# Linear attention and an MLP in one kernel: stripes 2 and 3 take k by v and the output product over the whole TensorE array, under a new order of the list

## The chip, the cores and the metric

The kernel runs on one core of one Trainium2 chip. The metric is device time in microseconds of one execution; lower is better. The engines are TensorE (PE, with its weight loads shown apart as PEld), VectorE (DVE), ScalarE (ACT), GpSimd (POOL) and the queue that issues most transfers (SP). Each has its own instruction stream, worked through in order, and semaphores hold an instruction until what it needs is there.

## The reference, cut to what matters

There are 4 batches and 8 heads, 768 positions, a head dimension of 64. The attention is linear, with a decay: within a block it is a masked product, and a state of 64x64 per head carries the earlier blocks.

```python
for b in range(nb):
    intra = np.einsum('bhic,bhjc->bhij', qb, kb) * Dmask[None]
    intra = np.einsum('bhij,bhjd->bhid', intra, vb)
    inter = np.einsum('bhid,bhde->bhie', qb * lam_pow[None], kv_state)
    out[:, :, sl] = intra + inter
    kb_dec = kb * rev_pow[None]
    kv_state = lam_block[None, :, None, None] * kv_state + np.einsum('bhsd,bhse->bhde', kb_dec, vb)
...
h = x @ w_in
g = np.where(pos, h, np.where(neg, 0.0, (h + beta) ** 2 / (4.0 * beta)))
return (g @ w_out).astype(np.float32)
```

The attention's output, 3072 rows of 512, is the x of the MLP: 512 to 2048 to 512, with a smooth ReLU between (beta is 1). The kernel takes blocks of 128 positions where the reference has 64; the result is the same function. Products are taken in bf16 and accumulated in float32.

## The kernel before

**Tiling.** The 24 blocks of 128 rows are cut into eight stripes of 4, 2, 3, 3, 3, 3, 3 and 3 blocks (`STRIPES`, line 25). The heads go in pairs, hp 0 to 3; a unit is a stripe and a pair, so `S21` is the scores of stripe 2, pair 1. A stripe's attention is followed by its MLP, in 16 parts of the hidden layer and one output block per block of rows.

**The order.** Nothing is scheduled by a tool. `ORDER` (lines 29 to 71) is a list of words, and the loop at line 574 issues the instructions of each word on their engines in that order. Each engine goes through its own words strictly in that order, so a word that waits holds every later word of its engine. The words:

- `L21k`: load k (or q, v) of stripe 2, half 1, issued by SP. `W0` to `W7`: the weights, issued by POOL (W0 to W3 a quarter of w_in each, W4 to W7 of w_out). `W4@L10q` makes the first transfer of the one wait until the last of the other has landed.
- `k21g`, `q21d`, `v21a`: scale k or q by its decay, or copy v, into bf16; the last letter is the engine (g POOL, d DVE, a ACT).
- `T`, `Q`: transpose k or q of a unit (on PE in stripes 0 to 3, by a DMA in 4 to 7); `t`, `u`: ACT takes the transposes out of PSUM.
- `S`, `s`: scores on PE, mask on DVE. `R`, `r`: k by v on PE (`att_r`, line 361), the state's step on DVE (line 404). `O`, `o`: output on PE (`att_o`, line 409), copied out by ACT. `X`: transpose of the output by a DMA (stripes 4 to 7).
- `P03`, `h03`: part 3 of stripe 0's hidden layer (PE, line 503) and its ReLU (ACT, line 526); `K` is the same for the first three parts, one pair of heads at a time. `A`: the rest of the activation for four parts (DVE, lines 482 to 485). `Y012`: part 2 of the four parts of output block 1 of stripe 0 (PE, line 535); `y` copies it out, `U` stores it.
- `B`: a mask. `E`: the table of decays for stripe 0's scan. `G`: zeros in a kq tile. `D2`: two matmuls on the identity whose result nobody reads (line 491).

**Two forms of the attention.** In stripes 0 to 3 two heads of 64 are packed into the array: k by v and the output product write PSUM partitions 0 to 63 for one head and 64 to 127 for the other, so they use half of the columns each (64 columns of weights, `128*64` in the trace), the state's part also half of the rows (`64*64`), the scores half of the rows (`64*128`):

```python
nc.tensor.matmul(po[p0:p0 + 64, c, :],
                 lhsT=d["vc"][:, hi, c, :], rhs=d["sc"][:, hi, c, :],
                 start=(c == 0), stop=(prior[c] is None), skip_group_check=True)
...
nc.tensor.matmul(po[p0:p0 + 64, c, :], lhsT=prior[c][p0:p0 + 64, :],
                 rhs=d["qT"][p0:p0 + 64, c * 128:(c + 1) * 128], ...)
```

In stripes 4 to 7 (`whole`) zeros stand between the heads in the tile of k, and every product uses the whole array (`128*128`); the state is then 128x128 with zeros off its two diagonal blocks, and the output comes out with rows on partitions, which the DMA of `X` transposes.

**PSUM.** There are four banks for the MLP (`pmm`, also taken by `D`), two for transposes, k by v and output (`pat`), two for one unit's scores (`psp`).

**The words around the change on POOL**, from the first weight load on: W0@L03v, W1@L01k, v03g, W2, W3@L03q, W4@L10q, v11g, q11g, W5, k13g, W6, W7, v12g, q20g. And on PE after stripe 0's first ten P words: P0b, P0c, Q12, Q10, T12, P0d, T10, P0f, T13, P0e, T11, S10, D1, Q13, D1, Q11, Y010.

Of the kernel before, what the change touches and what calls it, by code (L numbers as in the profile page):

```python
# [23 lines left out]

STRIPES = [(0, 0, 4), (0, 4, 2), (1, 0, 3), (1, 3, 3), (2, 0, 3), (2, 3, 3), (3, 0, 3), (3, 3, 3)]
# [4 lines left out]
D2 B1a E D1 D1 B0a D2 D2 L00q D1 L01v L02q L00k D2 L01k L03v q02g L00v k00a B3a q00g k01g L01q  # L30
Q00 L02v T00 D2 q01g v02g t00 u00 L02k Q02 T01 S00 L03q u02 t01 D1 L03k D1 B2a D2 Q01 s00 u01
v00d k02d S01 W0@L03v D2 s01 T02 R00 D2 D2 r00 L11q q03d t02 R02 W1@L01k v03g v01a O00 S02
L10v@W1 r02 k03d o00 R01 r01 s02 Q03 T03 t03 u03 D2 W2 W3@L03q O01 o01 S03 O02 q12d s03 R03 D1
r03 o02 K01 K02 L10q@W2 O03 o03 K00 K03 h01 L10k@W2 L11k@W1 h02 h00 P05 P03 P09 P0a h03 h05 h0a
W4@L10q P08 A00 P06 v11g q11g W5 h09 v10a P07 P04 h06 L11v@W3 k13g q10d h08 k11d P0b P0c Q12
k12d h07 Q10 T12 h0b P0d h04 L20q@W5 u12 t12 q13d k10d T10 P0f T13 u10 P0e L20k W6 t10 T11 h0d
t13 S10 D1 L21q W7 Q13 h0c A01 v12g q20g D1 v13d h0f h0e Q11 Y010 Y020 u13 s10 t11 u11 R11 R10
S11 Y030 s11 r11 r10 Y011 Y031 S12 O10 R12 A02 Y000 Y021 o10 Y012 R13 Y001 L20v@W1 A03 L21k@W1
r12 s12 Y032 r13 L30q Y022 O11 S13 L21v O12 k21a Y023 Y033 L31k L30k L31v k20g L31q o11 o12 y02
Q20 s13 Y013 y03 O13 Y002 v20g o13 u20 y01 q21g P12 h12 T20 k22g q22d q30g P10 P1a P15 h10 Q21  # L40
h1a U03 t20 P17 P11 h15 S20 R20 P13 k30g h17 k23d v21a L30v q23d Y003 u21 h13 T21 r20 h11 P14
P18 T22 s20 h14 t21 y00 v23g Q22 u22 A10 P16 O20 h16 v22d h18 D2 t22 o20 P1b P19 P1e A11 P1f T23
R21 h1b h19 S21 h1e h1f r21 q32g P1c s21 Q23 P1d h1d A12 h1c u23 Q30 v31g Y100 Y101 S22 t23 R23
Y110 k31a r23 T30 Y102 u30 Y111 Y112 s22 S23 k32a U02 L40k O21 v30g t30 o21 R22 A13 Y103 s23 r22
S30 O23 s30 v33g O22 o23 v32d Y113 o22 L40q R30 R31 P24 h24 r31 r30 G40 k33g q31d P20 R32 y11
# [12 lines left out]
L70k R53 r60 P45 S61 h45 y31 P4f X52 L70q O60 v63a o60 P4a P4e X51 h4f h4a r53 Y410 Y400 A41 O53
o53 q71g Y420 h4e A42 Y411 R61 A43 U32 Y421 Y401 Y412 Y402 R62 X53 s61 Y413 P57 k72a Y403 h57
T63 L70v k70g r61 r62 y41 P51 h51 P5a S62 s62 P50 O61 y40 v73d Y422 R63 P53 k73a h50 o61 h53 S63  # L60
h5a s63 k71g q70g P52 U40 v72d P58 Y423 T71 O62 h52 y42 P59 P54 h59 h54 T70 P56 h56 P5b r63 P55
O63 A50 S70 h55 o62 o63 q73d s70 P5d R73 P5f h58 r73 R72 U41 X61 U22 P5e h5d h5b h5f v70a h5e
U31 X62 P5c Y500 X63 A51 X60 A52 Y510 R70 h5c Y501 S71 Y511 P60 P63 h63 Y512 h60 Y502 A53 P68
q72g T73 r72 s71 Y503 Y513 P62 h68 v71g h62 T72 P61 y51 h61 S72 P67 R71 P6a P65 h67 h6a s72 r70
P6b h6b P66 U51 O72 y50 P69 A60 S73 r71 P6f o72 s73 h66 P64 X72 O71 h6f h69 P6d Y520 o71 Y521
h6d O70 P6c A62 o70 X71 h64 O73 Y522 h65 h6c P6e Y523 Y610 Y600 A61 o73 h6e A63 y52 X70 Y611
Y612 U42 Y601 Y602 X73 P75 Y613 Y603 y61 P78 P70 y60 h78 h75 P76 h76 P7b h7b P73 Y620 P71 U50
h73 h70 P72 U52 P7a U61 h71 P79 Y621 h72 h7a h79 Y622 A72 Y623 P74 h74 y62 P77 P7e h77 h7e P7d
P7f A70 P7c h7d h7f h7c U60 Y710 A71 Y700 Y711 Y701 Y712 U62 A73 Y713 Y702 Y703 y71 y70 U71 U70
Z72  # L70
# [8 lines left out]
def kernel(  # L79
# [63 lines left out]
    def load(s, n, which):  # L143
# [9 lines left out]
        if which == "q" and s < S_WH:  # L153
            return [nc.sync.dma_start(out=t.rearrange("p h c d -> p h (c d)"),
                                      in_=src.rearrange("h (p c) d -> p h (c d)", c=C))]
# [78 lines left out]

    kq_tiles = [const.tile([128, 9, 128], BF16, name=f"kq{i}") for i in range(NZ)]

    def kq_tile(u):
        return kq_tiles[(NP * u[0] + u[1]) % NZ]

    def set_zeros(u):  # L240
        C = shape(u[0])[0]
        z = kq_tile(u)[:, 0:2 * C, :].rearrange("p (c h) e -> p c h e", h=2)
        for hi in range(2):
            nc.gpsimd.memset(z[:, :, hi, (1 - hi) * D:(2 - hi) * D], 0.0)


# [10 lines left out]
    def att_cast(u, which, eng):  # L257

        s, hp = u
        C, T, first, last, whole = shape(s)  # L260
        src = raw[s, which][:, 2 * hp:2 * hp + 2, 0:C, :]
        d = st.setdefault(u, {})
        if which == "v":
            d["vc"] = bfp.tile([128, 2, CM, D], BF16, name="vc", tag="vc")
            dst = d["vc"][:, :, 0:C, :]
            if eng == "a":
                nc.scalar.copy(out=dst, in_=src)
            else:
                (nc.gpsimd if eng == "g" else nc.vector).tensor_copy(dst, src)  # L269
            return  # L270
        kq = d["kq"] = kq_tile(u)
        if which == "k" and whole:

            ap = list(kq[:, 0:2 * C, 0:D].ap)
            dst = bass.AP(kq.tensor, kq.offset, [ap[0], [128 + D, 2], [256, C], [1, D]])
        else:
            c0 = 0 if which == "k" else 2 * C if whole else C
            dst = kq[:, c0:c0 + C, :].rearrange("p c (h d) -> p h c d", h=2)
        row = 0 if which == "k" else Q1 if whole else {4: Q4, 2: Q2, 3: Q3}[C]
        inner = which == "q" and not whole  # L280
# [13 lines left out]

    def att_t(u, i):

        s, hp = u
        C, T, first, last, whole = shape(s)
        d = st[u]
        if "kqT" not in d:  # L300
            d["kqT"] = trp.tile([128, 9, 128], BF16, name="kqT", tag="kqT")
        if whole:
            nc.sync.dma_start_transpose(out=d["kqT"], in_=d["kq"].rearrange("p c e -> p (c e)"))
            return
# [18 lines left out]
    def att_s(u):  # L323

        s, hp = u
        C, T, first, last, whole = shape(s)
# [3 lines left out]
        for c in range(C):  # L330
            for hi in range(2):
                o = ps[:, hi, c * 128:(c + 1) * 128]
                if whole:
# [18 lines left out]
    def before(u):  # L352

        s, hp = u
        C, T, first, last, whole = shape(s)
# [4 lines left out]

    def att_r(u):

        s, hp = u
        C, T, first, last, whole = shape(s)
        d = st[u]
        n = C - 1 if last else C
        if whole:
# [5 lines left out]
        else:  # L373
            d["pk"] = pk = pat.tile([128, CM, D], F32, name="pk", tag="pat")
            d["ss"] = ssp.tile([128, CM, D], BF16, name="ss", tag="ss")
        for c in range(n):
            for hi in range(2):
                if whole:
                    nc.tensor.matmul(pk[:, c, hi, :],
                                     lhsT=d["kq"][:, 2 * c + hi, :], rhs=d["vc"][:, hi, c, :],  # L380
                                     start=True, stop=True)
# [4 lines left out]
                                 start=True, stop=True)  # L386

    def att_state(u):

        s, hp = u  # L390
        C, T, first, last, whole = shape(s)
# [7 lines left out]
        for c in range(C - 1 if last else C):  # L399
            kv = d["pk"][:, c, :, :].rearrange("p h e -> p (h e)") if whole else d["pk"][:, c, :]  # L400
# [7 lines left out]

    def att_o(u):

        s, hp = u
        C, T, first, last, whole = shape(s)
        d = st[u]
        if s not in x_tiles:
            x_tiles[s] = xpool.tile([128, KO, TM], BF16, name="xT", tag="xT")
        prior = [before(u)] + [d["ss"][:, :, c] if s == 0 else d["ss"][:, c, :]
                               for c in range(C - 1)]
        if whole:
            d["xn"] = xnp.tile([128, 3 * BLK], BF16, name="xn", tag="xn")
# [3 lines left out]
        for c in range(C):  # L423
            for hi in range(2):
                if whole:
# [10 lines left out]
        for c in range(C):  # L436
            if prior[c] is None:
                continue
            if whole:
# [10 lines left out]
    def att_out(u):  # L450

        s, hp = u
        C, T, first, last, whole = shape(s)
        d = st[u]
        if whole:
# [5 lines left out]
    def att_x(u):  # L461

        s, hp = u
        C, T = shape(s)[:2]
# [179 lines left out]
```

## Time and profile before

| what | value |
| --- | --- |
| time, median of 3 runs | 227.57 us (227.45 to 227.84) |
| the profiled execution's own time | 228.49 us |
| its span, first to last instruction | 226.8 us |
| mean granted TensorE clock | 0.985 |
| DMA | 35.95 MB, mean 159 GB/s |
| L503, hidden layer on PE | 500 matmuls, 91.1 us busy |
| L535, output layer on PE | 368 matmuls, 87.6 us busy |
| L526, ReLU on ACT | 128 instructions, 70.2 us busy |

How to read it: the span is cut into 40 equal slices, and a digit is the busy share of a slice in tenths. PEclk is the granted TensorE clock in the same slices. In a timeline a row has the start, the time to the end of the last of its instructions, engine, line, operation, tiles and shape, how many instructions were merged, and in brackets how long the engine had been idle and what ended that. The end of a matmul is modelled and overlaps the next one's start, so what a matmul takes of PE's stream is read from start to start. A row of a view by line has busy time, mean ns of one, and idle time before. In a view of stretches each engine has its busy time and count, and the last three numbers are the granted clock, the DMA share and GB/s.

### The profile page before, as it was taken

The numbers are of one execution on the slowest core, as the hardware profiler recorded it, in microseconds if no ns is written. First come the engines' busy times: TensorE is split into PE (matmuls) and PEld (weight loads), VectorE is DVE, ScalarE is ACT, GpSimd is POOL, SyncE is SP. The second block draws the span as 40 slices with busy tenths as digits, with TensorE's granted clock in tenths as the row PEclk, the third lists the DMA queues.
The fourth block names the chain that finished last, engine by engine and source line by source line (L and its number), as shares of the span: only waits on it lengthen the run. The fifth ranks groups of instructions, "written<-read, shape, count | busy, mean of one in ns | idle before, by whom it ended". The sixth has DMA issues, their size and how long they took to land.

```text
span 226.8 us, 4443 instructions
## 1 busy us (share of the span) xinstructions
PE 216.1 (95%) x1703; PEld 121.8 (54%) x1703; DVE 144.9 (64%) x233; ACT 125.9 (56%) x264; POOL 50.7 (22%) x89
## 2 busy tenths in 40 slices
PE   7389999999999999999999999999999999999994
PEld 2146444444775465555654666556654565455453
DVE  1059267792489767989399775991799486404930
ACT  5555487305986277985553666616681576074620
POOL 4672019123351435000313340024010000000000
PEclk9769999999999999999999999999999999999999
DMA  4999989999998699439999799999945103220112
GB/s 117 233 250 166 209 201 144 195 265 225 216 265 206 150 182 223 112 74 207 191 206 151 180 236 156 180 214 232 198 111 105 46 17 101 93 95 3 46 46 93
DMA packets 100630, 35.95 MB, mean 159 GB/s; under 512 B 89217, under 2 KB 97665, under 8 KB 100609
## 3 DMA queue, kind: packets, MB, share of 16 engines
q1 hardware_dynamic: 96384, 31.47, 63.9%
q0 software_dynamic: 4224, 4.19, 12.1%
q8 instruction: 13, 0.21, 0.4%
q14 instruction: 9, 0.07, 0.1%
HBM read 27.27 MB, written 6.29 MB: 148 GB/s over the span
## 4 chain that ended last, share of the span: by engine, by line
PE 73%; DMA 13%; SPq 5%; DVE 4%; ACT 1%; POOL 1%; issue 1%; DVEq 0%; POOLq 0%
PE py L535 31%; PE ph L503 28%; DMA w_in_sb<-in_moe_w_in_dram 5%; SPq L158 3%; DMA kqT<-kq 2%; DMA k_nat<-in_k_dram 2%; PE ps L334 2%; DMA xT<-xn 2%; DMA v_nat<-in_v_dram 2%; PE pt L310 2%; PE py L555 2%; PE po L432 1%; PE po L446 1%; PE ps L338 1%; DVE gT L485 1%; DVE ww L484 1%
## 5 line engine op out<-in xcount | busy, mean ns | idle before, releaser
L526 ACT ACTIVATE tt<-ph,one 128x384 bf16<-128x384 f32 (+2 forms) x128 | 70.2, 587 | 38.4 <-PE ph L503 25.4
L503 PE MATMUL ph<-xT,w_in_sb 128*128 128x384 bf16 (+2 forms) x500 | 91.1, 325 | 0.2
L535 PE MATMUL py<-w_out_sb,gT 128*128 128x512 bf16 x368 | 87.6, 379 | 0.5 <-DVE gT L485 0.5
L503 PEld LDWEIGHTS <-w_in_sb 128*128 128x128 bf16 x500 | 46.6, 98 | 30.3 <-DMA xT<-xn 0.6
L535 PEld LDWEIGHTS <-gT 128*128 128x128 bf16 x368 | 34.2, 98 | 36.3 <-DVE gT L485 1.5
L347 DVE TENSOR_TENSOR sc<-ps,mask 128x768 bf16<-128x768 f32 (+2 forms) x32 | 30.5, 953 | 30.1 <-PE ps L334 15.3
L485 DVE TENSOR_TENSOR gT<-ww,mm 128x1536 bf16<-128x1536 bf16 (+2 forms) x32 | 31.5, 985 | 1.2
L484 DVE TENSOR_TENSOR ww<-tt,mm 128x1536 bf16<-128x1536 bf16 (+2 forms) x32 | 31.2, 974 | 1.1
L482 DVE TENSOR_SCALAR mm<-tt 128x1536 bf16<-128x1536 bf16 (+2 forms) x32 | 18.1, 565 | 21.2 <-ACT tt L526 20.1
L292 POOL TENSOR_TENSOR kq<-q_nat,dec 128x384 bf16<-128x384 f32 (+2 forms) x19 | 18.1, 962 | 34.2 <-DMA q_nat<-in_q_dram 31.6
L543 ACT COPY osb<-py 128x512 f32<-128x512 f32 x23 | 13.4, 584 | 20.1 <-PE py L535 15.1
L269 POOL CAST vc<-v_nat 128x384 bf16<-128x384 f32 (+2 forms) x14 | 9.6, 684 | 52.3 <-PE po L440 28.0
L458 ACT CAST xT<-po 128x384 bf16<-128x384 f32 (+2 forms) x16 | 7.7, 482 | 13.7 <-PE po L446 13.6
L310 PE MATMUL pt<-ident,kq 128*128 128x128 bf16 x96 | 10.4, 238 | 4.3 <-POOL kq L292 3.9
L287 POOL TENSOR_SCALAR kq<-k_nat,dec 128x192 bf16<-128x192 f32 (+2 forms) x22 | 11.9, 553 | 5.8 <-DMA k_nat<-in_k_dram 5.8
L491 PE MATMUL pw<-ident 128*128 128x512 bf16 x31 | 11.8, 504 | 1.4 <-POOL ident masks.py:199 1.4
L310 PEld LDWEIGHTS <-kq 128*128 128x128 bf16 x96 | 8.1, 107 | 8.9 <-POOL kq L292 4.4
L283 ACT ACTIVATE kq<-k_nat,dec 128x192 bf16<-128x192 f32 (+1 forms) x22 | 8.9, 461 | 6.7 <-DVE sc L347 4.6
L404 DVE SCALAR_TENSOR_TENSOR sz<-sz,lam_blk,pk 128x128 bf16<-128x128 bf16 x32 | 11.0, 345 | 0.9
L456 ACT CAST xn<-po 128x384 bf16<-128x384 f32 x16 | 7.5, 482 | 5.3 <-PE po L440 5.3
L320 ACT COPY kqT<-pt 128x384 bf16<-128x384 bf16 (+2 forms) x16 | 7.9, 492 | 4.1 <-PE pt L310 4.1
L318 ACT COPY kqT<-pt 128x384 bf16<-128x384 bf16 (+2 forms) x16 | 7.8, 488 | 3.8 <-PE pt L310 3.8
(63 smaller groups left out, 142.7 us busy)
## 6 DMA issues: line engine op xcount, KB each, us to landing
out_dram<-osb SPq DMA_DIRECT2D x23, 256.0 KB, 2.6
q_nat<-in_q_dram SPq DMA_DIRECT2D x18, 256.0 KB, 4.3
v_nat<-in_v_dram SPq DMA_DIRECT2D x24, 128.0 KB, 4.2
k_nat<-in_k_dram SPq DMA_DIRECT2D x24, 128.0 KB, 4.5
k_nat<-in_k_dram SPq DMA_DIRECT2D x12, 256.0 KB, 4.3
v_nat<-in_v_dram SPq DMA_DIRECT2D x12, 256.0 KB, 4.4
w_in_sb<-in_moe_w_in_dram POOLq DMA_DIRECT2D x4, 512.0 KB, 10.8
w_out_sb<-in_moe_w_out_dram POOLq DMA_DIRECT2D x4, 512.0 KB, 7.9
```

The lines of the kernel that those rows point to most:

```text
L287: nc.gpsimd.tensor_scalar(dst[:, hi, :, :], src[:, hi, :, :], dec[:, row, 2 * hp + hi:2 * hp + hi + 1], 0.0, AX.mult, AX.add)
L292: (nc.gpsimd if eng == "g" else nc.vector).tensor_tensor(dst, src, decay(row, 2 * hp, C, inner), op=AX.mult)
L310: nc.tensor.transpose(out=d["pt"][:, i, c, :], in_=d["kq"][:, i * C + c, :], identity=ident)
L347: nc.vector.tensor_tensor(out=d["sc"][:, :, 0:C, :], in0=d["ps"][:, :, 0:T].rearrange("p h (c i) -> p h c i", c=C), in1=_ins(mask[:, 2 * h ...
L482: nc.vector.tensor_scalar(mm, tt, 0.5, 1.0, AX.mult, AX.min)
L484: nc.vector.tensor_tensor(ww, tt, mm, op=AX.subtract)
L485: nc.vector.tensor_tensor(g[:, 4 * a:4 * a + 4, 0:T], ww, mm, op=AX.mult)
L491: nc.tensor.matmul(pw, lhsT=ident, rhs=_ins(ident[:, :], 1, 4), start=True, stop=True)
L503: nc.tensor.matmul(ph[:, 0:T], lhsT=w_in_sb[:, ko, ni * 128:(ni + 1) * 128], rhs=x_tiles[s][:, ko, 0:T], start=(ko == 0), stop=(ko == KO - 1))
L526: nc.scalar.activation(out=t_tiles[s, ni // 4][:, ni % 4, 0:T], in_=p_tiles[s, ni][:, 0:T], func=AF.Relu, bias=one[:, 0:1])
L535: nc.tensor.matmul(y_tiles[s, m], lhsT=g_tiles[s][:, ko, m * 128:(m + 1) * 128], rhs=w_out_sb[:, ko, :], start=(ko == 0), stop=(ko == FO - 1))
L543: nc.scalar.copy(out=osb, in_=y_tiles[s, m])
```

## The change

A string `FORMS` names the form of each stripe: p packed, f new, w whole as before. Stripes 2 and 3 become f. In form f the scores and transposes stay packed as they were, but k by v and the output product use the whole array. For that v is kept in one of four permanent tiles with 64 columns of zeros between the two heads, and k, once scaled, is copied into such a tile by a new word `z` (eight of them: z20a, z21a, z22a, z32a, z33a on ACT, z23g, z30g, z31g on POOL). A slice of 128 columns that begins at one head or at the zeros is then that head's weights with the other head's columns zero. The state of these stripes becomes 128x128. A new word `J` writes zeros into the middles of the eight tiles, once, on POOL.

Beside this the list has a new order up to word P48 of stripe 4 (from there on it is the same), the product of the activation is written over its input instead of a tile of its own, the v tiles are permanent in every stripe, and an x tile is laid out by its stripe's own width. `NU` is 1, so that the code for two pairs in one tile does nothing here.

On POOL the words are now: q02g, E, v02g, W0, q03g, W2, W1@L00v, W3, v03g, W4@L10v, J, W5@L02k, q11g, q10g, q13g, k11g, W6@L02q, W7@L00k, v13g, q21g. On PE after stripe 0's `K` words: P03, P08, P0b, P06, P07, P04, P05, P09, P0a, Q12, Q10, P0f, P0d, P0e, T10, T12, P0c, S10, D2, T11, T13, Q13, Q11, Y030. On ACT around there: h05, h0a, h04, u10, k10a, t10, t12, u12, h0e, v10a, h0f, h0c. L10v now waits for W2 instead of W1, both times the second weight load that is issued.

```diff
+FORMS = "ppffwwww"
...
-r03 o02 K01 K02 L10q@W2 O03 o03 K00 K03 h01 L10k@W2 L11k@W1 h02 h00 P05 P03 P09 P0a h03 h05 h0a
-W4@L10q P08 A00 P06 v11g q11g W5 h09 v10a P07 P04 h06 L11v@W3 k13g q10d h08 k11d P0b P0c Q12
+O00 v03g O01 o00 k03d D1 o01 T03 s02 L10v@W2 W4@L10v J Q03 t03 u03 R02 r02 S03 R03 O02 o02 D2
+r03 s03 K00 L10q@W1 K02 O03 W5@L02k q11g K01 q12d q10g o03 K03 h02 P03 L10k@W2 h01 P08 q13g L11k
...
+    vc_all = [const.tile([128, CM, 3, D], BF16, name=f"vc{i}") for i in range(4)]
+    kz_all = [const.tile([128, 3, 3, D], BF16, name=f"kz{i}") for i in range(NKZ)]
...
+    def set_middles():
+        for t in vc_all + kz_all:
+            nc.gpsimd.memset(t[:, :, 1, :], 0.0)
+
+    def middle(t, c, hi):
+        return t[:, c, hi:hi + 2, :].rearrange("p z e -> p (z e)")
...
-            d["vc"] = bfp.tile([128, 2, CM, D], BF16, name="vc", tag="vc")
-            dst = d["vc"][:, :, 0:C, :]
+            d["vt"] = vc_free.pop(0)
+            d["vc"] = dst = d["vt"][:, 0:C, 0:3:2, :].rearrange("p c h e -> p h c e")
...
+    def att_z(u, eng):
+        d["kz"] = kz_free.pop(0)
+        dst = d["kz"][:, 0:C, 0:3:2, :]
+        src = d["kq"][:, 0:C, :].rearrange("p c (h e) -> p c h e", h=2)
+        if eng == "a":
+            nc.scalar.copy(out=dst, in_=src)
+        else:
+            (nc.gpsimd if eng == "g" else nc.vector).tensor_copy(dst, src)
...
-                if whole:
+                if fm != "p":
                     nc.tensor.matmul(pk[:, c, hi, :],
-                                     lhsT=d["kq"][:, 2 * c + hi, :], rhs=d["vc"][:, hi, c, :],
-                                     start=True, stop=True)
+                                     lhsT=(d["kq"][:, 2 * c + hi, :] if fm == "w" else
+                                           middle(d["kz"], c, hi)),
+                                     rhs=d["vc"][:, hi, c, :], start=True, stop=True)
...
+                if fm == "f":
+                    nc.tensor.matmul(po[:, c, :], lhsT=middle(d["vt"], c, hi),
+                                     rhs=d["sc"][:, hi, c, :],
+                                     start=(c == 0 and hi == 0),
+                                     stop=(prior[c] is None and hi == 1),
+                                     skip_group_check=True)
+                    continue
...
+            if fm == "f":
+                nc.tensor.matmul(po[:, c, :], lhsT=prior[c],
+                                 rhs=d["qT"][:, c * 128:(c + 1) * 128],
+                                 start=False, stop=True, skip_group_check=True)
+                continue
...
-        ww = spool.tile([128, 4, TM], BF16, name="ww", tag="ww")[:, :, 0:T]
-        nc.vector.tensor_tensor(ww, tt, mm, op=AX.subtract)
-        nc.vector.tensor_tensor(g[:, 4 * a:4 * a + 4, 0:T], ww, mm, op=AX.mult)
+        nc.vector.tensor_tensor(tt, tt, mm, op=AX.subtract)
+        nc.vector.tensor_tensor(g[:, 4 * a:4 * a + 4, 0:T], tt, mm, op=AX.mult)
```

More of the change, by code (lines that the diff above doesn't have):

```diff
@@ L34 @@
-r03 o02 K01 K02 L10q@W2 O03 o03 K00 K03 h01 L10k@W2 L11k@W1 h02 h00 P05 P03 P09 P0a h03 h05 h0a
-W4@L10q P08 A00 P06 v11g q11g W5 h09 v10a P07 P04 h06 L11v@W3 k13g q10d h08 k11d P0b P0c Q12
[L36 to L45, printed above, removed]
@@ new lines @@
+k13d L20k@W5 h05 P0f h0a h04 k12d P0d u10 k10a P0e v13g T10 t10 T12 t12 P0c L20q u12 S10 L21k@W6
+h0e D2 v10a h0f T11 T13 L20v Q13 A01 h0c Q11 Y030 u13 A02 s10 Y020 h0d t13 Y000 u11 Y010 t11
+Y011 R10 v12a v11a r10 R11 S11 Y031 Y021 s11 Y001 S12 r11 R13 q21g O10 o10 Y022 Y032 A03 r13 s12
+Y033 S13 R12 O11 Y012 y03 s13 r12 k20a o11 O13 k21a O12 q20d Y023 L21v@W1 o13 o12 z20a v21d P10
+v20g y02 T20 T21 Q20 h10 P19 t21 P18 k23d Y002 L21q@W5 v22d Y013 q22g z21a t20 u20 h18 R20 P11
+S20 k22d y01 h19 Q21 P13 h11 P12 u21 L31k q23d P16 L30k z22a Y003 T22 h13 h12 U02 P17 P15 L31q
@@ L259, in att_cast @@
         s, hp = u
-        C, T, first, last, whole = shape(s)
+        C, T, first, last, fm = shape(s)
         src = raw[s, which][:, 2 * hp:2 * hp + 2, 0:C, :]
@@ L271, in att_cast @@
         kq = d["kq"] = kq_tile(u)
-        if which == "k" and whole:
+        if which == "k" and fm == "w":
             ap = list(kq[:, 0:2 * C, 0:D].ap)
@@ L276, in att_cast @@
         else:
[L277 removed]
+            c0 = 0 if which == "k" else 2 * C if fm == "w" else C
             dst = kq[:, c0:c0 + C, :].rearrange("p c (h d) -> p h c d", h=2)
[L279 to L280 removed]
+        row = 0 if which == "k" else Q1 if fm == "w" else {4: Q4, 2: Q2, 3: Q3}[C]
+        inner = which == "q" and fm != "w"
         if eng == "a" and not inner:
@@ L325, in att_s @@
         s, hp = u
-        C, T, first, last, whole = shape(s)
+        C, T, first, last, fm = shape(s)
         d = st[u]
@@ L354, in before @@
         s, hp = u
-        C, T, first, last, whole = shape(s)
+        C, T, first, last, fm = shape(s)
         if first:
@@ L386, in att_r @@
                                  start=True, stop=True)
+        if fm == "f":
+            kz_free.append(d["kz"])
     def att_state(u):
         s, hp = u
-        C, T, first, last, whole = shape(s)
+        C, T, first, last, fm = shape(s)
         d = st[u]
@@ L452, in att_out @@
         s, hp = u
-        C, T, first, last, whole = shape(s)
+        C, T, first, last, fm = shape(s)
         d = st[u]
-        if whole:
+        if fm == "w":
             nc.scalar.copy(out=d["xn"], in_=d["po"][:, 0:C, :, :].rearrange("p c h d -> p (c h d)"))
```

145 lines of the change are left out of this document (87 added, 58 removed).

## The prediction, made before the changed kernel was run

> **What bounds the kernel now.** I read the page first: its span, busy times and slices, and the chain.
>
> ```profile
> span 226.8 us, 4443 instructions
> PE 216.1 (95%) x1703; PEld 121.8 (54%) x1703; DVE 144.9 (64%) x233; ACT 125.9 (56%) x264; POOL 50.7 (22%) x89
> PE   7389999999999999999999999999999999999994
> PEclk9769999999999999999999999999999999999999
> PE 73%; DMA 13%; SPq 5%; DVE 4%; ACT 1%; POOL 1%; issue 1%; DVEq 0%; POOLq 0%
> ```
>
> PE is full from the fifth slice (about 23 us) to the end, at full clock; no other engine is over 64%. So from there on the end moves by what PE gains or loses: work taken from its stream, or a hole made in it. Next comes the timeline of PE, from the first stripe's hidden layer to the first matmul of its output layer.
>
> ```profile
> 27.14 8.80 PE L503 MATMUL ph<-xT,w_in_sb 128*128 128x512 bf16 x40
> 35.77 0.39 PE L310 MATMUL pt<-ident,kq 128*128 128x128 bf16 x4
> 36.56 0.29 PE L310 MATMUL pt<-ident,kq 128*128 128x128 bf16 x2 [0.41 <-DVE kq L292]
> ...
> 39.71 0.29 PE L338 MATMUL ps<-kqT 64*128 64x128 bf16 x4
> 39.93 0.39 PE L491 MATMUL pw<-ident 128*128 128x512 bf16 x1
> ...
> 40.59 0.59 PE L535 MATMUL py<-w_out_sb,gT 128*128 128x512 bf16 x2
> ```
>
> A 512-column matmul takes (35.77-27.14)/40 = 0.216 us of the stream; a four-matmul P word 0.86. The one hole is at 36 us, where a transpose of stripe 1 waits for a scaled k or q. Those casts share POOL with the weight loads, so POOL's timeline over the same stretch matters, together with the landing of the load that L10v issues.
>
> ```profile
> 33.05 0.74 POOL L232 DMA_DIRECT2D w_out_sb<-in_moe_w_out_dram  x1 [14.72 <-DMA q_nat<-in_q_dram]
> 33.78 0.41 POOL L269 CAST vc<-v_nat 128x256 bf16<-128x256 f32 x1
> 34.15 0.81 POOL L292 TENSOR_TENSOR kq<-q_nat,dec 128x256 bf16<-128x256 f32 x1
> 34.91 0.80 POOL L232 DMA_DIRECT2D w_out_sb<-in_moe_w_out_dram  x1
> ```
>
> ```profile
> L160 SPq DMA_DIRECT2D v_nat<-in_v_dram x2: 368/438/507, 25.8 to 26.2; - x2
> DMA to landing us min/median/max: 5.7/5.7/5.8
> ```
>
> W4@L10q holds POOL itself: 14.72 us idle, and the casts behind it start only after 33 us. L10v, issued when the second weight load has landed (25.8 us), lands at 26.2 + 5.8 = 32.0.
>
> **Part 1: k by v and output on the whole array.** The timeline of PE shows stripes 2 and 3 in the packed form, and stripe 4 in the whole-array form.
>
> ```profile
> 60.39 0.34 PE L338 MATMUL ps<-kqT 64*128 64x128 bf16 x6
> ...
> 75.60 0.28 PE L384 MATMUL pk<-vc,kq 128*64 128x64 bf16 x6
> 75.81 1.04 PE L535 MATMUL py<-w_out_sb,gT 128*128 128x512 bf16 x4
> ...
> 85.62 0.50 PE L310 MATMUL pt<-ident,kq 128*128 128x128 bf16 x6
> 86.06 0.34 PE L338 MATMUL ps<-kqT 64*128 64x128 bf16 x6
> 86.33 1.47 PE L503 MATMUL ph<-xT,w_in_sb 128*128 128x384 bf16 x8
> ...
> 90.56 0.36 PE L432 MATMUL po<-sc,vc 128*64 128x128 bf16 x6
> 91.13 1.15 PE L503 MATMUL ph<-xT,w_in_sb 128*128 128x384 bf16 x6
> ```
>
> ```profile
> 113.04 0.50 PE L334 MATMUL ps<-kqT 128*128 128x128 bf16 x6
> 113.38 1.03 PE L535 MATMUL py<-w_out_sb,gT 128*128 128x512 bf16 x4
> 114.24 0.34 PE L426 MATMUL po<-vc,sc 128*128 128x64 bf16 x6
> 114.42 0.28 PE L440 MATMUL po<-sz,kqT 128*128 128x128 bf16 x2
> ```
>
> Starts are what count, since matmuls overlap. On the whole array a 128-column matmul takes (113.38-113.04)/6 = 0.057 us and a 64-column one (114.42-114.24)/6 = 0.03. Entering a packed shape costs extra: six transposes from 85.62 should end at 85.96, and the scores start at 86.06, 0.10 late; leaving costs as much. One unit's packed output takes 91.13-90.56 = 0.57, plus 0.10 to enter; whole, it is 9 x 0.057 = 0.51 with nothing to enter. A packed k by v takes 75.81-75.60 = 0.21 plus its entry; whole, 6 x 0.03 = 0.18. Scores stay packed, 0.27 + 0.10 each.
>
> Stripes 2 and 3 have twelve packed runs between 60.39 and 91.13. From the expected end of the matmul before to the next whole-array start they take 0.58, 0.61, 0.58, 0.58, 1.10, 1.40, 0.34, 0.73, 0.55, 0.37, 1.52 and 0.67, in all 9.05 us. After: 8 scores x 0.37 = 2.95, 40 k by v x 0.03 = 1.16, 68 output matmuls x 0.056 = 3.81: 7.92. **Minus 1.13 us of PE.** Bounds: 0 if loading weights with zeros showed, 1.5 if less of the entry is left.
>
> Here a rule speaks against the change. The Trainium skill, TensorEngine Tiling (Array Packing), section Theoretical Speedup, gives packing up to twice the speed where a dimension is 64 or less. By that alone the 4.97 us of whole-array streaming replace about half of that, and the sum below would be about 232. The same page, Key Properties, says that a change of tiling mode drains TensorE; the 0.10 us at 86.06 agrees, and at runs of six matmuls the drain eats the packing.
>
> What pays for the zeros lies beside PE:
>
> ```profile
> L244 POOL MEMSET kq<- 128x192 bf16 x10 | 2.3, 258 | 4.0 <-DVE kq L292 3.2 <-PE pt L310 0.4 <-POOL kq L244 0.3
> L404 DVE SCALAR_TENSOR_TENSOR sz<-sz,lam_blk,pk 128x128 bf16<-128x128 bf16 x32 | 11.0, 345 | 0.9
> L404 DVE SCALAR_TENSOR_TENSOR ss<-ss,lam_blk,pk 128x64 bf16<-128x64 bf16 x20 | 5.4, 278 | 1.2 <-PE pk L384 0.8
> L320 ACT COPY kqT<-pt 128x384 bf16<-128x384 bf16 x8 | 3.9, 488 | 1.5 <-PE pt L310 1.5
> L526 ACT ACTIVATE tt<-ph,one 128x512 bf16<-128x512 f32 x16 | 10.1, 692 | 2.1 <-PE ph L503 0.7 <-PE ph L517 0.7 <-issue 0.5
> ```
>
> Twenty state steps are wider by 0.067 us: 1.3 us of DVE, covered by its 36% idle. Eight z copies, five on ACT, three on POOL, at about 0.49 (the 488 ns copy is nearest): 2.4 us of ACT, hidden under P and Y words while four PSUM banks absorb the delay; uncovered, all 2.4 would show. From P10 to P30 ACT's list grows from 60 to 70 words (about 30 to 35 us by their rows) against 40 us of PE. I take 0.4 us of new holes there, bounds 0 and 2.4. The product written over tt instead of ww, the permanent v tiles and the x tile's new view issue as many instructions as before: nothing.
>
> **Part 2: the new order on POOL.** POOL's queue becomes W0, q03g, W2, W1, W3, v03g, W4@L10v, J, W5, q11g, q10g, q13g, k11g, W6, W7. L10v still follows the second weight load, so it lands at about 32.0; with a quarter us for the wait to end, my estimate, and 0.74 for the issue, W4 is done at 33.0. J, moved in right behind that wait, is eight memsets: four like the 258 ns row, four a third larger, 0.26 to 0.34 each, so 2.1 to 2.4; I take 2.3, until 35.3. W5 0.80: 36.1. q11g 0.81: 36.9. q10g 0.81: **37.7**. Before, v11g and q11g followed W4 at once, and q10 was scaled on DVE.
>
> PE reaches Q10 earlier. If the hidden layer starts near 27.14 as now, nine P words (36 x 0.216) and Q12 end at 35.0. Q10 waits until 37.8: a hole of **2.8 us**. Behind it in PE's order stand three P words, T10, T12, P0c, S10, D2, four transposes and all Y words; on ACT u10, k10a, t10, t12, u12 and h0e wait with it. An earlier start of the first stripe would only widen the hole: POOL sets its end.
>
> From Q10 to the first Y: transposes 0.11 + 0.22 + 0.45, four P words 3.46, S10 0.32 (39.71 to 39.93 plus entry), D2 0.43, in all 4.99: 42.8. P0f, P0d, P0e and P0c hold all four PSUM banks, so D2 needs the one that h0e frees; behind T10 (40.5) ACT first does three copies of stripe 1, 256 wide, 0.4 each as an estimate from the 0.49 of 384, and a 0.69 us relu, which puts D2 at 42.7 and the first Y at 43.6. I take 43.3 against 40.59: **plus 2.7 us** (2.2 to 3.3).
>
> **Part 3: the other moves.** From P48 on the lists agree. Two warming words fall away after the Y words begin:
>
> ```profile
> 64.61 0.60 PE L491 MATMUL pw<-ident 128*128 128x512 bf16 x2
> 65.06 1.91 PE L503 MATMUL ph<-xT,w_in_sb 128*128 128x256 bf16 x16
> ...
> 84.53 0.39 PE L491 MATMUL pw<-ident 128*128 128x512 bf16 x1
> 84.98 0.81 PE L503 MATMUL ph<-xT,w_in_sb 128*128 128x384 bf16 x4
> ```
>
> 0.45 each: **minus 0.9** (0.45 if the second covers a wait that stays). SP's order of the first loads changes, but they carry the same bytes, and W0 still waits for L02v's cast, now by queue order. L20k@W5 is no later than L20q@W5 was.
>
> **The sum** is made on this execution's own 226.8 us span, which ended as a run of 228.49; the three runs have a median of 227.57, 0.92 below it. 2.7 - 1.13 - 0.9 + 0.4 = +1.1 on the span: 227.9, and on the median **228.7 us**. The low ends of hole, streams and holes later (0.5, 0.4, 0.4), taken as independent, give 0.75 less; the high ends of hole and warming words (0.6, 0.45) and 0.4 of later holes 0.85 more: 227.9 to 229.6. The far high ends of streams and ACT are rivals D and E.
>
> **Rivals.** (B) The hole never opens. It needs q10g by 35.0, hence L10v landed by 29.2 instead of 32.0; from there each microsecond later costs one. For it: the weights in flight delay L10v, and their order changed. Against it: the same number of weight loads is queued when it is issued. Then even the 0.5 us hole at 36 goes: -0.5 - 1.13 - 0.9 + 0.1 = -2.4: 225.2, faster.
>
> (C) The hole drops PE's clock. In the first 16 us this happened:
>
> ```profile
> 5.00:9.00 4.00, 0.90 (x4) 0.15 (x1) 0.33 (x2) 2.83 (x8) 2.11 (x3) 0.97 1.03 228
> 9.00:12.00 3.00, 2.16 (x14) 1.60 (x15) 0.00 (x0) 1.88 (x5) 1.69 (x3) 0.50 1.06 244
> ```
>
> PE was busy 0.90 of 4 us there, so idle for 3.1, and the granted clock (third number from the end) was 0.50 through the next 3 us. A 2.8 us hole is a little shorter; if it suffices, 3 us at half rate cost 1.5 more: 230.2. The Trainium skill, TensorE: Matmul & The Clock Gate, Part 1, has the rate halve after an idle window of about 3.4 us. By that rule the hole stays just short.
>
> (D) ACT becomes the bound between P10 and P30 and shows 1.5 us more than I took: 230.2. For it the 35 of 40 us; against it the four banks.
>
> (E) The whole array saves nothing (229.8), or the unpacked streams take twice the packed ones' time: 2.5 more instead of 1.13 less, 232.3. For it: twice as many columns stream one after the other. Against it: 0.51 for 0.57 in the rows above, with weights in stripe 4 as wide and half zero. The packing rule cited above would end here.
>
> **Chances.** Forecast 0.44, B 0.32, C 0.10, D 0.09, E 0.05. This kernel's runs cannot tell less than 0.2% (0.45 us) from no change. Faster: 0.28, B without its upper edge. Same: 0.13, the edges of B and the forecast. Slower: 0.59. With B and the slower cases the range runs from 224.8 to 231.0; the forecast's own is the 227.9 to 229.6 above.
>
> **What would show it.** A POOL wait ended by v_nat near 32, eight memsets behind it, a PE hole of 2 to 3 us before a transpose at 35 to 38 ended by POOL's q cast, the first Y near 43.3; k by v of stripes 2 and 3 at 0.18 us per six, twelve runs worth 7.9 us; full clock after 16 us. Wrong would be a first Y before 41, or holes over 1 us between P10 and P30.

## The result and the profile after

| | before | after |
| --- | --- | --- |
| median, same chip | 227.7 us (227.15 to 228.46, 10 runs) | 226.53 us (225.86 to 228.09, 10 runs) |
| ratio, 95% interval | | 0.995 (0.9928 to 0.9973) |
| the profiled execution | 228.49 us | 225.86 us |
| its span | 226.8 us | 224.1 us |

The changed kernel is faster by 0.5%, 1.1 us. The forecast, 228.7 us, said slower. The two profiled executions stand 2.6 us apart, more than the medians: the one of after is the fastest of its ten, the one of before is slower than all ten of before in the table. Of the runs below, two of e3's twelve were in a slower state of the chip and are left out.

The page of the changed kernel, its span, busy times, slices and chain:

```profile
span 224.1 us, 4412 instructions
PE 214.2 (96%) x1683; PEld 122.7 (55%) x1683; DVE 150.8 (67%) x236; ACT 128.8 (57%) x276; POOL 45.6 (20%) x90
PE   6498999999999999999999999999999999999994
PEclk9769999999999999999999999999999999999999
PE 87%; DVE 5%; DMA 2%; ACT 2%; SPq 2%; issue 1%; DVEq 0%; ACTq 0%
```

PE is still the bound and still at full clock from the fourth slice on; DVE and ACT are busy 6 and 3 us longer than before, and still lie beside it. POOL's timeline over the words that Part 2 of the prediction is about (start, time, engine, line, operation; in brackets the idle time ahead and what ended it):

```profile
30.97 0.74 POOL L236 DMA_DIRECT2D w_out_sb<-in_moe_w_out_dram  x1 [12.04 <-DMA v_nat<-in_v_dram]
31.70 1.09 POOL L260 MEMSET vc<- 128x256 bf16 x4
32.70 0.88 POOL L260 MEMSET kz<- 128x192 bf16 x4
33.51 0.76 POOL L236 DMA_DIRECT2D w_out_sb<-in_moe_w_out_dram  x1
34.27 1.99 POOL L310 TENSOR_TENSOR kq<-q_nat,dec 128x256 bf16<-128x256 f32 x3
```

The wait and its releaser are the ones that the prediction named, but it ends at 31 and not at 32.25, and `J` takes 1.8 us (31.70 to 33.51). PE's timeline, first up to the first Y, then some words of stripes 2 and 3:

```profile
27.44 8.01 PE L561 MATMUL ph<-xT,w_in_sb 128*128 128x512 bf16 x36
35.28 0.55 PE L334 MATMUL pt<-ident,kq 128*128 128x128 bf16 x4
35.67 2.75 PE L561 MATMUL ph<-xT,w_in_sb 128*128 128x512 bf16 x12
...
40.13 0.59 PE L549 MATMUL pw<-ident 128*128 128x512 bf16 x2 [0.41 <-ACT tt L584]
40.56 0.61 PE L334 MATMUL pt<-ident,kq 128*128 128x128 bf16 x8
41.01 4.48 PE L593 MATMUL py<-w_out_sb,gT 128*128 128x512 bf16 x20
...
69.41 0.34 PE L416 MATMUL pk<-vc,kz 128*128 128x64 bf16 x6
69.58 1.89 PE L593 MATMUL py<-w_out_sb,gT 128*128 128x512 bf16 x8
...
73.34 0.50 PE L472 MATMUL po<-sc,vc 128*128 128x128 bf16 x6
73.67 0.28 PE L493 MATMUL po<-kqT,sz 128*128 128x128 bf16 x2
73.78 0.33 PE L334 MATMUL pt<-ident,kq 128*128 128x128 bf16 x3
```

The predicted hole of 2.8 us before stripe 1's transposes is not there: four transposes take 0.39 from start to start (35.28 to 35.67) where they need 0.22, so 0.16 is lost. Six k by v of stripe 2 take 0.17, and eight output matmuls 0.44 (73.34 to 73.78).

**Where the time came from.** From the first Y matmul to the last, PE's stream can be added up from start to start: each whole-array matmul at its undisturbed time (0.216, 0.163, 0.109, 0.056 or 0.029 us by its columns), each packed run from the expected end of the matmul before it to the next whole-array start, and what is left over as holes (the rows add up to within 0.02).

| us | before | after | difference |
| --- | --- | --- | --- |
| start of the first Y | 40.59 | 41.01 | +0.42 |
| packed and whole-array runs of stripes 2, 3 | 9.05 | 7.92 | -1.13 |
| packed runs of stripe 1 | 3.58 (5 runs) | 3.24 (4 runs) | -0.34 |
| warming words | 0.65 | 0 | -0.65 |
| holes | 1.88 | 0.91 | -0.97 |
| first Y to last Y, all | 182.84 | 179.77 | -3.07 |

Of the holes, 0.23 stood behind the second warming word of before and went with it. Another 0.95 lay late in before, in words that the change leaves alone, as here in its timeline of PE:

```profile
140.50 0.81 PE L503 MATMUL ph<-xT,w_in_sb 128*128 128x384 bf16 x4
141.45 0.51 PE L334 MATMUL ps<-kqT 128*128 128x128 bf16 x6
...
171.18 1.03 PE L535 MATMUL py<-w_out_sb,gT 128*128 128x512 bf16 x4
172.33 1.47 PE L503 MATMUL ph<-xT,w_in_sb 128*128 128x384 bf16 x8
```

Four matmuls of 0.163 from 140.50 end at 141.15, so 0.30 is lost; four of 0.216 from 171.18 end at 172.04, 0.29 lost. Whether these belong to the kernel or to that one execution is a question for the experiments.

### The profile page after: what moved, and what is told of

It reads as the page before. It is cut to its first block, busy times and chain, and to the rows that moved or that the text cites. A ratio compares the mean times of both kernels' runs of the same rounds, so it can differ in the third digit from the quotient of the medians.

```text
span 224.1 us, 4412 instructions
## 1 busy us (share of the span) xinstructions
PE 214.2 (96%) x1683; PEld 122.7 (55%) x1683; DVE 150.8 (67%) x236; ACT 128.8 (57%) x276; POOL 45.6 (20%) x90
## 4 chain that ended last, share of the span: by engine, by line
PE 87%; DVE 5%; DMA 2%; ACT 2%; SPq 2%; issue 1%; DVEq 0%; ACTq 0%
PE py L593 33%; PE ph L561 33%; PE pw L549 3%; PE pt L334 2%; PE ps L358 2%; DMA v_nat<-in_v_dram 2%; PE ps L362 2%; PE py L613 2%; PE pk L416 2%; DVE tt L542 1%; DVE gT L543 1%; PE po L472 1%; PE po L479 1%; PE ph L575 1%; SPq L162 1%; PE po L504 1%
## 5 line engine op out<-in xcount | busy, mean ns | idle before, releaser
L543 DVE TENSOR_TENSOR gT<-tt,mm 128x1536 bf16<-128x1536 bf16 (+2 forms) x32 | 31.7, 990 | 1.2
L542 DVE TENSOR_TENSOR tt<-tt,mm 128x1536 bf16<-128x1536 bf16 (+2 forms) x32 | 31.3, 979 | 1.1
L310 POOL TENSOR_TENSOR kq<-q_nat,dec 128x384 bf16<-128x384 f32 (+2 forms) x17 | 14.8, 890 | 48.4 <-DMA q_nat<-in_q_dram 35.6
L444 DVE SCALAR_TENSOR_TENSOR sz<-sz,lam_blk,pk 128x128 bf16<-128x128 bf16 x48 | 16.4, 346 | 1.7 <-PE pk L416 0.5
L287 POOL CAST vc<-v_nat 128x384 bf16<-128x384 f32 (+2 forms) x12 | 7.1, 588 | 48.1 <-PE po L498 31.5
L310 DVE TENSOR_TENSOR kq<-k_nat,dec 128x384 bf16<-128x384 f32 (+2 forms) x11 | 7.5, 689 | 7.3 <-PE pk L416 4.6
L334 PEld LDWEIGHTS <-kq 128*128 128x128 bf16 x96 | 7.1, 106 | 8.2 <-DVE kq L310 2.7
L301 ACT ACTIVATE kq<-k_nat,dec 128x192 bf16<-128x192 f32 (+2 forms) x26 | 10.6, 464 | 0.9 <-PE pk L416 0.9
L342 ACT COPY kqT<-pt 128x384 bf16<-128x384 bf16 (+2 forms) x16 | 7.7, 490 | 3.5 <-PE pt L334 3.5
L305 POOL TENSOR_SCALAR kq<-k_nat,dec 128x192 bf16<-128x192 f32 (+1 forms) x16 | 8.2, 528 | 2.9 <-PE pt L334 2.9
```

The lines of the kernel that those rows point to most:

```text
L310: (nc.gpsimd if eng == "g" else nc.vector).tensor_tensor(dst, src, decay(row, 2 * hp, C, inner), op=AX.mult)
L334: nc.tensor.transpose(out=d["pt"][:, i, c, :], in_=d["kq"][:, i * C + c, :], identity=ident)
L444: nc.vector.scalar_tensor_tensor(out=d["ss"][:, c, :], in0=prev, scalar=lam_blk[:, hp:hp + 1], in1=kv, op0=AX.mult, op1=AX.add)
L542: nc.vector.tensor_tensor(tt, tt, mm, op=AX.subtract)
L543: nc.vector.tensor_tensor(g[:, 4 * a:4 * a + 4, 0:T], tt, mm, op=AX.mult)
```

## The experiments

Each was timed beside the kernel before on its own chip; e1 to e4 share one chip, e5 to e8 another.

**e6, the kernel before again** (no edit), and **e8, the changed kernel again** (no edit): what varies from one execution to the next.

> The kernel before once more, for a second profile. Theory (executions differ before the first Y, by when the second weight load lands; from the first Y on they are alike): first Y at 39.6 to 40.6 us, and 182 to 183 us from the first Y to the last. Rival (the two profiles shown differ by more than the change): a last stretch below 181 us.

> The changed kernel once more, for a second profile and a time beside the others. Theory (from the first Y on PE's stream is fixed, before it the landing of L10v decides): 179.8 us from the first Y to the last as in the first profile, a hole before Q10 between 0.1 and 1.2 us that is the larger the later L10v lands. Rival (the first profile was typical): hole 0.1 to 0.2 us.

e6 ran 225.95 us once, faster than any of 22 timed runs of before on that chip (median 226.92, 226.05 to 228.25). Its timeline of PE, from the first stripe's hidden layer and at the first Y:

```profile
25.91 8.80 PE L503 MATMUL ph<-xT,w_in_sb 128*128 128x512 bf16 x39
...
38.91 1.90 PE L535 MATMUL py<-w_out_sb,gT 128*128 128x512 bf16 x7
```

(In the traces of e5 to e8 the records of 22 to 24 matmuls are missing, hence 39 where 40 ran.) The first Y stands at 38.91, 1.7 us ahead of the first profile of before, with the same list and ahead of all that was expected; from there to the last Y it takes 181.96, and the holes at 141, 170 and 172 are gone. They were that execution's. e8, the changed kernel again, gave 0.9969 (0.9949 to 0.9989, 12 runs, median 226.2): 0.7 us faster than before. In its profile (226.85 us) POOL and PE read

```profile
31.98 0.74 POOL L236 DMA_DIRECT2D w_out_sb<-in_moe_w_out_dram  x1 [12.72 <-DMA v_nat<-in_v_dram]
32.71 1.09 POOL L260 MEMSET vc<- 128x256 bf16 x4
...
34.53 0.76 POOL L236 DMA_DIRECT2D w_out_sb<-in_moe_w_out_dram  x1
35.28 1.99 POOL L310 TENSOR_TENSOR kq<-q_nat,dec 128x256 bf16<-128x256 f32 x3
37.26 2.40 POOL L305 TENSOR_SCALAR kq<-k_nat,dec 128x128 bf16<-128x128 f32 x2
```

```profile
27.84 8.01 PE L561 MATMUL ph<-xT,w_in_sb 128*128 128x512 bf16 x35
35.69 0.28 PE L334 MATMUL pt<-ident,kq 128*128 128x128 bf16 x2
36.56 0.28 PE L334 MATMUL pt<-ident,kq 128*128 128x128 bf16 x2 [0.60 <-POOL kq L310]
...
42.02 4.26 PE L593 MATMUL py<-w_out_sb,gT 128*128 128x512 bf16 x18
```

Here the load lands late, as forecast, and the hole opens: two transposes from 35.69 end at 35.80, the next start at 36.56, so 0.76 us; the profile names POOL's q cast. The first Y is at 42.02, and from there to the last Y it takes 179.77 again. So the part behind the first Y repeats to 0.01 us in these two, and what varies between executions of this kernel lies ahead of it. With the list of before, the first Y stood at 40.59, 38.91 and, in e5 below, 39.48: on the mean 39.66. With the list of after at 41.01, 42.02 and, in e1, 41.02: 41.35. The new start costs 1.7 us on the mean of three. Only a part of that is the hole. The first stripe's hidden layer, which the prediction took as starting when it did before, starts at 27.14, 25.91 and 26.61 with the list of before and at 27.44, 27.84 and 26.84 with that of after: 0.8 later on the mean. Whether the earlier words cause that, or chance, no run settles. From there to the first Y it takes 13.45, 12.99 and 12.87 before and 13.57, 14.18 and 14.19 after: 0.9 more, in which the holes of 0.16, 0.76 and 0.77 have 0.6.

**e3, J twice**: the hole made as large as it was forecast.

```diff
-... L10v@W2 W4@L10v J Q03 ...
+... L10v@W2 W4@L10v J J Q03 ...
```

> The changed kernel with J twice in its place, 1.8 us more on POOL. Theory (no slack is left in front of Q10): PE's hole before Q10 grows to about 2 us, the first Y comes 1.6 to 1.8 us later and the end with it: about 228.2 us. Rival (the hole at 39.5 us and later waits take it up): 0.8 us more at most, under 227.4 us.

It took 228.06 us (10 runs, 227.21 to 229.97), 1.0071 (1.0041 to 1.0101) of before; against e8's ratio that is 1.0% or 2.3 us more for 1.8 us of memsets, where 1.6 to 1.8 was expected. Its timeline of PE, and busy times in two stretches (PE, PEld, DVE, ACT, POOL, each with its count, then granted clock, DMA share, GB/s):

```profile
35.82 0.27 PE L333 MATMUL pt<-ident,kq 128*128 128x128 bf16 x2
38.87 0.28 PE L333 MATMUL pt<-ident,kq 128*128 128x128 bf16 x2 [2.78 <-POOL kq L309]
...
44.33 1.89 PE L592 MATMUL py<-w_out_sb,gT 128*128 128x512 bf16 x8
```

```profile
36.00:39.00 3.00, 0.22 (x5) 0.13 (x4) 1.51 (x3) 1.58 (x3) 3.00 (x6) 1.00 1.08 177
39.00:42.00 3.00, 3.00 (x19) 1.48 (x18) 2.93 (x3) 1.07 (x4) 3.00 (x3) 1.00 0.89 144
```

The hole is 2.94 us from start to start, the first Y 2.3 us behind e8's, and all of it shows in the time: POOL's chain does set PE here, with no slack. The 0.5 beyond the memsets is POOL's too. Its q casts read

```profile
37.07 3.40 POOL L309 TENSOR_TENSOR kq<-q_nat,dec 128x256 bf16<-128x256 f32 x3
```

against 1.99 for three in e8; q10's own cast, the second, takes 1.16 where it took 0.64, with DVE busy beside it (see the last section). PE was busy 0.22 of 3 us and the clock stayed 1.00 behind it, so rival C falls. The Trainium skill, TensorE: Matmul & The Clock Gate, Part 1, has the clock fall after an idle window of about 3.4 us; 2.78 us that left it alone agrees.

**e2, J ahead of the wait**: the memsets in POOL's idle time.

```diff
-... O00 v03g O01 ... L10v@W2 W4@L10v J Q03 ...
+... O00 v03g J O01 ... L10v@W2 W4@L10v Q03 ...
```

> The changed kernel with J moved ahead of W4, into POOL's idle time. Theory (POOL now delivers q10 just in time; the hole before Q10 is 0.16 us): q10 is scaled 1.8 us sooner, only that 0.16 us can go: within 0.4 us of the changed kernel, 226.1 to 226.6 us. Rival (the prediction's reading: J behind the wait holds PE by its whole length): 1.8 us faster or more, under 225 us.

225.12 us (6 runs), 0.9934 (0.9908 to 0.996); the hole is gone, the first Y at 40.39, 179.77 behind it as before. By the ratios that is 0.4 and 0.8 us ahead of the changed kernel (0.995 and 0.9969), about its hole of 0.2 to 0.8 us, though the intervals overlap. The traces are clearer: from the hidden layer's start to the first Y it is 13.40 here, and 13.57 and 14.18 with the holes of 0.16 and 0.76. So in the changed kernel most of the 1.8 us of `J` is run while PE is still busy with the first stripe's hidden layer.

**e1, the new list with stripes 2 and 3 packed**: the list without the form.

```diff
-FORMS = "ppffwwww"
+FORMS = "ppppwwww"
...
-... o13 o12 z20a v21d P10 ...
+... o13 o12 v21d P10 ...
```

(and so for the other seven z words; `J` writes the four v tiles twice, so that it stays about as long, 2.0 us for 1.8, and the state has a tile per stripe).

> The changed kernel with stripes 2 and 3 packed again, in the same order; the z words fall away, J still writes eight tiles' worth of zeros on POOL. Theory (PE's stream sets the end from 24 us on): the twelve packed runs take about 9.0 us again instead of about 7.9, so 1.1 to 1.3 us more than the changed kernel, about 227.7 us. Rival (the z copies on ACT cost what the whole array saves): no slower than the changed kernel, 226.5 us or less.

228.68 us (6 runs), 1.0084 (1.006 to 1.0108): slower than before by 1.9 us, and than the changed kernel by 1.3% (0.995) or 1.15% (0.9969). Its timeline of PE at the words shown of after above:

```profile
68.96 1.03 PE L592 MATMUL py<-w_out_sb,gT 128*128 128x512 bf16 x4
69.92 0.28 PE L421 MATMUL pk<-vc,kq 128*64 128x64 bf16 x6
70.14 1.90 PE L592 MATMUL py<-w_out_sb,gT 128*128 128x512 bf16 x8
...
73.11 1.03 PE L592 MATMUL py<-w_out_sb,gT 128*128 128x512 bf16 x4
74.06 0.36 PE L484 MATMUL po<-sc,vc 128*64 128x128 bf16 x6
74.35 0.30 PE L503 MATMUL po<-kqT,sr 64*64 64x128 bf16 x4
74.58 0.34 PE L333 MATMUL pt<-ident,kq 128*128 128x128 bf16 x3
```

Four Y matmuls from 68.96 end at 69.82; k by v starts at 69.92 and the next Y at 70.14: 0.31 for what takes 0.17 in form f. The output takes 73.97 to 74.58, 0.61 for 0.44. In all, the packed runs of stripes 2 and 3 take 9.95 us here, in 19 runs, where before's list has the same words in 12 runs and 9.05 us: the new list sets packed words apart, and each run pays its entry. In the new list the form is therefore worth 9.95 - 7.92 = 2.03 us of stream, and first to last Y is 182.16 against 179.77. The time says 2.6 to 3.0, well over the 1.1 to 1.3 that was expected. Of the 2.39 between the two profiles, 0.52 is one hole of e1 at 171.6, in words that the change leaves alone; what else the timed difference holds stays open.

**e4, the form in the list of before**: its list with the z words behind the `t` or `k` word of their unit, and `J` ahead of `O01`, before W4's wait.

```diff
-... W3@L03q O01 ... U03 t20 P17 ...
+... W3@L03q J O01 ... U03 t20 z20a P17 ...
```

> The list of before, with stripes 2 and 3 in the new form: each z right behind its t word (or k word) on the engine it has in the changed kernel, J ahead of W4. Theory (the form is worth 1.1 to 1.3 us of PE whatever the order): about 226.5 us, and the twelve runs at about 7.9 us. Rival (the gain is the order's: warming words dropped, fewer late waits): 227.7 us or more, as before.

226.3 us (12 runs), 0.9966 (0.9941 to 0.999): 0.8 us faster than before. The streams give the same -1.13, and the time less than the 1.1 to 1.3 that was expected. This list was not made for the form; in its timeline of PE

```profile
67.24 0.60 PE L560 MATMUL ph<-xT,w_in_sb 128*128 128x256 bf16 x4
68.27 0.33 PE L333 MATMUL pt<-ident,kq 128*128 128x128 bf16 x3 [0.43 <-DVE sz L443]
...
127.17 2.11 PE L560 MATMUL ph<-xT,w_in_sb 128*128 128x384 bf16 x12
129.76 0.51 PE L357 MATMUL ps<-kqT 128*128 128x128 bf16 x6 [0.47 <-DMA kqT<-kq]
```

a transpose waits 0.59 for a state step (four matmuls of 0.109 from 67.24 end at 67.68), and three smaller holes stand at 65.8, 80.0 and 84.0, the last behind the warming word as in before; first to last Y is 182.39. The hole at 129, behind a DMA, lies where nothing was edited; this profile's execution took 227.13 us, 0.8 over the median, so some of these holes may be its own. So the form alone brings 0.8 us, the new list alone costs about 1.9, and the two together bring 0.7 to 1.1, no more than the form alone. The new list pays only with the form, and no gain of its own is shown: with `J` ahead of the wait, as e4 has it, e2 is 1.5 us faster than before, but the two intervals overlap.

**e5, before without its last two warming words.**

```diff
-... v22d h18 D2 t22 ... h22 D1 P2a ...
+... v22d h18 t22 ... h22 P2a ...
```

> The kernel before without its last two warming words (D2 behind h18, D1 behind h22), three matmuls that compute nothing. Theory (PE is full there, so each costs its 0.216 us of stream): 0.4 to 0.65 us less than before. Rival (they stand in time in which PE would wait anyway, as the 0.23 us wait behind the second one suggests): within 0.3 us of before.

225.78 us (11 runs), 0.9945 (0.9924 to 0.9966): 1.25 us faster (0.8 to 1.7), more than expected. First to last Y is 181.37, against 182.84 and 181.96 in the two profiles of before, so the traces give 0.6 to 1.5. How much of it is these words, at 0.65 of stream and the 0.23 hole behind them, and how much a list that happens to fall better, stays open. The time is as much as the whole change brings. No run has the form in the list of before without these words, so whether that, with no new order at all, would do as well as e2 is not shown.

**e7, what the readings add up to**: the changed kernel with `J` ahead of the wait, q10g ahead of q11g, and without `D2` behind S10, which waits for a bank.

```diff
-... O00 v03g O01 ... W4@L10v J Q03 ... W5@L02k q11g K01 q12d q10g o03 ... h0e D2 v10a ...
+... O00 v03g J O01 ... W4@L10v Q03 ... W5@L02k K01 q12d q10g q11g o03 ... h0e v10a ...
```

> The changed kernel with three moves: J ahead of W4, q10g ahead of q11g, and without the D2 behind S10, which waits 0.47 us for a PSUM bank and takes 0.43. Theory (the first Y is set by POOL's q cast and by that D2): first Y near 39.5 us, 0.6 to 1.5 us less than the changed kernel. Rival (the first Y waits for the same bank without D2, or for W4): 0.5 us less at most.

```profile
34.95 0.39 PE L333 MATMUL pt<-ident,kq 128*128 128x128 bf16 x4
35.17 2.75 PE L560 MATMUL ph<-xT,w_in_sb 128*128 128x512 bf16 x12
...
39.63 4.50 PE L592 MATMUL py<-w_out_sb,gT 128*128 128x512 bf16 x19
```

224.23 us (6 runs), 0.9883 (0.9853 to 0.9914): it beats both, and the changed kernel by 1.5 to 2.0 us by the ratios, at or over the upper end of what was expected. On PE there is no wait between Q12 and the first Y, which stands at 39.63, where before's list has it on the mean; from there it takes 179.80. So the start is where the new list lost what its form had gained.

## Why the prediction was wrong, step by step

**Part 2 failed: "first Y at 43.3", plus 2.7 us.** It measured +0.4 in the first pair of profiles and +1.7 on the mean of three, and the term that was mis-sized is the hole of 2.8 us before stripe 1's transposes: it measured 0.16, 0.76 and, in e1, 0.77. The order of events was right (the wait ended by v_nat, the eight memsets, the cast that ends PE's wait); sizes were not:

| | predicted | after | e8 |
| --- | --- | --- | --- |
| POOL's W4 starts, after v_nat's landing | 32.25 | 30.97 | 31.98 |
| W4, `J`, W5 | 0.74, 2.3, 0.80 | 0.73, 1.81, 0.76 | 0.73, 1.82, 0.75 |
| q11g and q10g together, the first two of three casts | 1.62 | 1.22 | 1.23 |
| q10 ready, two casts behind W5, about | 37.7 | 35.5 | 36.5 |
| PE ready for Q10 | 35.0 | 35.39 | 35.80 |
| hole | 2.8 | 0.16 | 0.76 |
| from Q10's start to the first Y | 5.5 | 5.46 | 5.46 |

The hole is the difference of two moments on two engines, and both were off towards each other. In e8, where the load lands when it was forecast to (0.3 us off), POOL is 1.2 us earlier by that, a `J` shorter by 0.5 and casts shorter by 0.4, and PE 0.8 later, mostly because the hidden layer started at 27.84 and not at 27.14; 2.8 less 2.0 is the 0.8 that was seen. In the first profile of after the second weight load also landed 1.2 us sooner, at 24.5 for 25.7, and L10v was issued with it, at 24.51 for 25.75 (timeline of SP's queue):

```profile
24.51 0.92 SPq L164 DMA_DIRECT2D v_nat<-in_v_dram  x2
```

Next to nothing of the hole was left. `J` was costed at the mean of 258 ns of one old memset form, with a third more for the larger tiles; the four larger ones took 0.25 each from start to start, the smaller ones 0.20. The last row, with `D2` behind S10 waiting 0.41 for the bank that h0e frees, came out as worked out.

The step also stood against one profile of before, whose first Y, at 40.59, was the latest of the three seen. And one row was misread on the way: the wait at 36 us in before was ended by DVE's k cast (`<-DVE kq L292`), not by a cast that shares POOL with the weight loads; no term of the sum rests on it.

**Part 1 held to the hundredth**: -1.13, 9.05 to 7.92; k by v 0.17 per six. What it missed is that the new list, which sets the packed words apart, gains more by the form: e1 shows it packed at 9.95. A -0.34 was missed as well: the new list has stripe 1's packed words in four runs and not five. Rival E falls. The gain of up to twice that the Trainium skill, TensorEngine Tiling (Array Packing), section Theoretical Speedup, gives for packing does not show at these lengths: the rows of e1 and after have 0.31 packed for 0.17, and 0.61 for 0.44.

**Part 3**: the warming words were put at -0.9; 0.65 of stream and the 0.23 hole behind them make 0.88. **The +0.4 of new holes** between P10 and P30 is one hole of 0.28 at 80.5. Rival D falls: no hole there is over 0.29, with DVE busy 42.0 and ACT 35.5 of 52 us between 41 and 93.

**The sum.** The forecast was +1.1 on the span, the pair of profiles gave -2.65. Of the 3.75 between them Part 2 is 2.3, before's late holes, which did not recur, 0.95, stripe 1's runs 0.34, and the last 0.2 for the most part new holes that stayed under 0.4. Against means of executions it reads: +1.7 at the start, -2.6 behind it (182.40, the mean of 182.84 and 181.96, to 179.77): -0.9, between the two timed differences of 1.1 and 0.7. By this reading the forecast is 2.0 off, 1.0 of it in Part 2 and 1.0 behind the first Y, where -1.6 was forecast: stripe 1's 0.34, half of before's late holes, and about 0.2 in smaller terms. The result lies between the forecast and rival B, whose hole "never opens": B's condition, q10g by 35.0, was missed by 0.5 and 1.5 us, but PE came later too. The prediction's own sign of being wrong, a first Y before 41, was not seen, by a hundredth (41.01). The range, 224.8 to 231.0, held the time; the chances leaned to the wrong side.

## What to carry to other kernels

A stall made by a slower queue is the difference of two arrivals: work out each with its own spread over executions before pricing it, and expect only the excess to show. A packed form must be priced by its runs, and so by the list around it: here runs of six and ten matmuls take longer packed than on the whole array, and the whole-array form is worth 1.13 us of PE's stream in the list of before and 2.03 in the new one, which sets the words apart. Initial writes that wait for nothing belong ahead of a queue's waits, not behind.

## What the hardware showed that was not expected

- **A packed run costs about 0.10 us to enter**, for a run of six matmuls as for one of ten (e1 at 69.92 and 74.06, above), so that short runs lose what packing saves.
- **POOL's casts and DVE's work are slow beside each other.** No run changes only this; the rows show it side by side. Two k casts on POOL take 2.40 us in e8 (37.26, above) and 0.72 in after (36.25). In those two stretches DVE was busy 2.26 of 2.33 us and 0.00 of 0.67:

```profile
37.27:39.60 2.33, 2.33 (x16) 1.20 (x14) 2.26 (x4) 1.04 (x5) 2.33 (x3) 1.00 1.20 191
```

```profile
36.25:36.92 0.67, 0.67 (x5) 0.29 (x3) 0.00 (x0) 0.67 (x3) 0.67 (x3) 1.00 1.24 199
```

  It goes both ways: DVE's two casts of 128x256 in after, at 33.6 to 36, as POOL starts its own, take 427 and 1796 ns:

```profile
L310 DVE TENSOR_TENSOR kq<-k_nat,dec x2: 427/1112/1796, 33.6 to 34.0; 128x256 bf16<-128x256 f32 x2
```

  The Trainium skill, GPSIMD Engine Reference, section Key points, says that GpSimd shares its SBUF interfaces with VectorE and contends with VectorE's instructions of two SBUF inputs; DVE's two casts are such, and the rows agree. The prediction gave casts one price.
- **The start varies by microseconds, the rest less.** L10v is issued between 23.8 us (e6) and 25.8 (before) and lands 5.7 to 6.0 later each time; from the first Y to the last, the five profiles of after's list in form f (after, e2, e3, e7, e8) take 179.77 to 179.80, the two of before 182.84 and 181.96.
